# A retention-and-feed-forward kernel: v of the first two batches loaded as bf16 by partition quarters and put in order on TensorE, and two blocks of the first product begun by halves

## The chip, the cores and the metric

The kernel runs on one core of one Trainium2 chip. The metric is device time in microseconds (us) of one execution; the time of a kernel is the median of several executions. A core has five engines with queues of their own: TensorE (PE, whose weight loads are listed apart as PEld), VectorE (DVE), ScalarE (ACT), GpSimd (POOL) and SyncE (SP). They run side by side and wait for one another through semaphores. Transfers are issued on POOL or SP and carried out by 16 DMA engines. Matrix products read their operands from the on-chip memory SBUF (128 partitions) and write to the accumulators in PSUM.

## The reference

```python
def _attn_ref(q, k, v):                      # (8 batches, 8 heads, 576 tokens, 64)
    scores = 1.0 / np.sqrt(64) * np.matmul(q, k.transpose(0, 1, 3, 2))
    gamma = 1.0 - 2.0 ** (-5.0 - np.arange(H))
    Dmat = np.where(rel >= 0, gamma[:, None, None] ** rel, 0.0)   # rel = row - column
    return np.matmul(scores * Dmat, v)

def _moe_ref(x, w_in, w_out):                # x (4608, 512), w_in (512, 2048), w_out (2048, 512)
    h = x @ w_in
    sp = np.where(h > 20.0, h, np.log1p(np.exp(np.minimum(h, 20.0))))
    return (h * np.tanh(sp)) @ w_out

def reference(q, k, v, moe_w_in, moe_w_out):
    x = _attn_ref(q, k, v).transpose(0, 2, 1, 3).reshape(B * S, H * D)
    return _moe_ref(x, moe_w_in, moe_w_out)
```

Each head is attention with a decay in place of a softmax: the weight of token j for token i is the score times gamma to the power i - j. Because nothing is normalised, a chunk of tokens can be computed from its own scores and a running state, the sum of k times v over the tokens before it. The result goes through two products with the function Mish between them.

## The kernel before

The 4608 tokens are cut into 36 chunks of 128, and four chunks make a tile of 512 tokens, so there are nine tiles. The first two tiles are the first 128 tokens of batches 0 to 3 and of batches 4 to 7; the other seven hold the rest in order. For every tile the kernel makes xT, the attention output with features on the partitions (4 x 128 features by 512 tokens). Then comes G1: sixteen blocks f (`g1`), each four products of 128x128 weights from w_in with 512 columns of xT, summed in a PSUM bank named hp, after which ACT applies Mish and writes gT. Then G2 (`g2_first`, `g2`): for each chunk, sixteen products of gT with w_out, summed, copied and stored. The attention work of a later tile is laid between the products of an earlier one. The order on every engine is written out by hand, and each engine's queue is in order: an instruction that waits holds all behind it.

Tile 0 has nothing before it that could cover its attention work, so the kernel begins with a stretch in which TensorE has little to do. It runs as follows (line numbers of the kernel before).

- POOL issues the loads of k, q and v of batches 0 to 3 (`load_first_qk`, L106; `load_first_v`, L117) and of w_in (`load_w_in`, L86), in the order written; SP issues q of batches 0 and 1. q and k come eight tokens to a row, 128 rows to a batch, and are cast to bf16 on the way, except on SP, which brings fp32. v comes as fp32 in pairs of batches, one token to a partition, 16 pieces of 64 values in each. Between the first loads POOL fills the tables of indices (L129 to L137) from which DVE makes the exponents of the decay (`dmask`, L150), the unit matrix (`ident`, L152) and `ex` (L600). ACT takes the exponentials (L598 to L602).
- `keep_warm` runs products of zeros on TensorE; their results are not used.
- `f_transpose` (L193, copies at L198) turns q and k of a pair of batches; `f_scores` (L212) multiplies them and DVE multiplies by the decay (L216, tile sm).
- `f_v` (L226) casts v to bf16 on ACT, POOL or DVE; `f_out` (L242) multiplies it with the masked scores, and a copy writes xT (L246), the last one on DVE.
- G1 of tile 0 begins (L513; with `halved` set, some products are split into two of 256 columns, L518).

While G1 of tile 0 runs, POOL scales v of batches 0 to 3 by the decay (`f_state`, L254, tile v0s), which with k of the same tokens (`cast_k0`, L262, cast from fp32) later gives the first state of each batch (L388). POOL's loads use eight semaphores in turn, so that a load's issue waits for the landing of the load eight before it.

## Time and profile before

| | |
|---|---|
| median of 3 runs | 301.16 us (300.12 to 302.53) |
| profiled execution | 301.52 us, of which span 299.7 us |
| busy share: DVE / ACT / POOL | 46% / 45% / 46% |
| moved by DMA | 47.44 MB, mean 158 GB/s |
| first product of G1 | at 17.02 us |
| v of batches 0, 1 | issued at 5.74 us, 6.97 us to landing |
| v of batches 2, 3 | issued at 6.93 us, 7.9 us to landing |

The span is the time from the first to the last instruction of one profiled execution; the execution's own time lies 1.8 us above it. The profile's page lists busy time by engine, the span in forty slices, the DMA queues, the chain of work that ended last, the costliest groups of instructions and the DMA issues. Groups read as: line, engine, operation, written tile, read tiles, shapes, count, then busy time and mean length. The trace answers further questions: who waited for whom, the instructions in order of time, and busy time by stretch. Ends of matmuls are modelled, so the start times of matmuls are the firmer numbers.

### The profile page before, as it was taken

To read this page: it belongs to the slowest core of one execution; us is meant where nothing else is said; L and a number is where in the kernel's file an instruction comes from. 1 tells how busy PE (TensorE), PEld (TensorE's weight loads), DVE (VectorE), ACT (ScalarE), POOL (GpSimd) and SP (SyncE) were. 2 spreads that over 40 slices of the span, in tenths; PEclk is the share of its full clock that TensorE was granted. 3 is DMA by queue.
4 is the path that set the end of the run, shared out by engine and by line. 5 is a ranking of instruction groups with operands and counts; after the bars stand their busy time and mean duration, and the time that the engine had idled before them with its cause. 6 is when DMAs were issued, how large, how long until landed. Compare 5 with 4: busy or idle time off the path is not lost.

```text
span 299.7 us, 7937 instructions
## 1 busy us (share of the span) xinstructions
PE 289.6 (97%) x3454; PEld 158.0 (53%) x3492; DVE 136.9 (46%) x234; ACT 135.1 (45%) x221; POOL 136.9 (46%) x184
## 2 busy tenths in 40 slices
PE   8889999999999999999999999999999999999995
PEld 3456787555455545456655454545454544444443
DVE  5813447597839527462646453536373312010011
ACT  5657226876557553534363434343435342433200
POOL 8596846767474297190927555817440000000000
PEclk9999999999999999999999999999999999999999
DMA  7999999999999649999897989797922110110121
GB/s 153 210 206 205 205 238 220 338 221 203 245 227 225 139 137 205 169 188 190 198 189 176 181 155 231 136 214 168 191 72 70 37 37 35 37 35 35 52 90 70
DMA packets 39618, 47.44 MB, mean 158 GB/s; under 512 B 21792, under 2 KB 28448, under 8 KB 39584
## 3 DMA queue, kind: packets, MB, share of 16 engines
q0 software_dynamic: 14896, 32.25, 51.6%
q1 hardware_dynamic: 24544, 14.49, 22.6%
q8 instruction: 27, 0.44, 0.7%
q10 hardware_dynamic: 144, 0.20, 0.2%
q14 instruction: 7, 0.06, 0.1%
HBM read 38.80 MB, written 9.44 MB: 161 GB/s over the span
## 4 chain that ended last, share of the span: by engine, by line
PE 92%; DMA 2%; issue 2%; POOL 2%; ACT 0%; DVE 0%; POOLq 0%
PE hp L513 41%; PE ops L513 30%; PE hp L518 6%; PE ops L518 3%; DMA gT<-in_v_dram 2%; PE sc L333 2%; PE hp L464 1%; PE sc L313 1%; PE sc L388 1%; PE hp L447 1%; PE hp L573 1%; PE st L518 1%; POOL gT L106 1%; PE st L388 1%; PE sc L190 1%
## 5 line engine op out<-in xcount | busy, mean ns | idle before, releaser
L513 PE MATMUL hp<-xT,w_in_t 128*128 128x512 bf16 (+1 forms) x508 | 127.8, 377 | 1.4 <-DVE gqk L650 0.3
L529 ACT ACTIVATE gT<-hp 128x512 bf16<-128x512 f32 x144 | 86.2, 599 | 92.2 <-PE hp L513 87.6
L513 PE MATMUL ops<-w_out_t,gT 128*128 128x512 bf16 x412 | 102.0, 379 | 2.0 <-issue 1.9
L513 PEld LDWEIGHTS <-w_in_t 128*128 128x128 bf16 x526 | 51.1, 98 | 54.8 <-issue 1.5
L513 PEld LDWEIGHTS <-gT 128*128 128x128 bf16 x480 | 45.7, 98 | 52.2
L581 DVE COPY res<-ops 128x512 f32<-128x512 f32 x28 | 19.3, 690 | 92.4 <-PE ops L513 92.4
L294 DVE TENSOR_TENSOR qks<-qkraw,gqk 128x512 bf16<-128x512 f32 x56 | 36.8, 714 | 3.6 <-DMA qkraw<-in_k_dram 3.6
L482 POOL COPY held<-qkT 128x1 bf16<-128x1 bf16 x18 | 5.4, 299 | 59.8 <-DMA qkT<-qks 59.8
L275 POOL DMA_DIRECT2D qkraw<-in_q_dram x24 | 21.4, 890 | 11.7 <-ACT gT L529 8.0
L275 POOL DMA_DIRECT2D vraw<-in_v_dram x24 | 21.2, 883 | 3.8 <-DMA vpair<-in_v_dram 3.0
L275 POOL DMA_DIRECT2D qkraw<-in_k_dram x24 | 21.2, 883 | 2.7 <-DMA w_out_t<-in_moe_w_out_dram 1.5
L476 DVE CAST xT<-hp 128x512 bf16<-128x512 f32 x13 | 9.0, 692 | 27.4 <-PE hp L464 19.7
L476 ACT CAST xT<-hp 128x512 bf16<-128x512 f32 x14 | 8.2, 586 | 29.0 <-PE hp L464 20.5
L301 POOL TENSOR_TENSOR vs<-vraw,gv 128x512 bf16<-128x512 f32 x18 | 18.9, 1075 | 1.2 <-PE hp L447 1.1
L424 DVE TENSOR_TENSOR total<-sc,total 128x256 f32<-128x256 f32 x40 | 16.9, 422 | 1.0
L339 DVE TENSOR_TENSOR sm<-sc,mask 128x1024 bf16<-128x1024 f32 x14 | 17.0, 1216 | 0.7 <-PE sc L333 0.7
L518 PEld LDWEIGHTS <-gT 128*128 128x128 bf16 x160 | 15.3, 98 | 3.2
L518 PE MATMUL hp<-xT,w_in_t 128*128 128x256 bf16 x108 | 16.2, 273 | 0.0
L518 PEld LDWEIGHTS <-w_in_t 128*128 128x128 bf16 x108 | 10.5, 98 | 6.5
L427 ACT CAST ssb<-total 128x768 bf16<-128x768 f32 (+3 forms) x13 | 11.7, 898 | 1.7 <-DVE total L424 1.6
L513 PE MATMUL hp<-w_out_t,gT 128*128 128x512 bf16 x49 | 12.0, 379 | 0.2 <-issue 0.2
L518 PE MATMUL ops<-w_out_t,gT 128*128 128x256 bf16 x76 | 10.0, 273 | 0.1
(118 smaller groups left out, 254.8 us busy)
## 6 DMA issues: line engine op xcount, KB each, us to landing
out_dram<-res SPq DMA_DIRECT2D x31, 256.0 KB, 4.3
qkraw<-in_q_dram POOLq DMA_DIRECT2D x24, 256.0 KB, 6.6
qkraw<-in_k_dram POOLq DMA_DIRECT2D x24, 256.0 KB, 6.9
vraw<-in_v_dram POOLq DMA_DIRECT2D x24, 256.0 KB, 7.7
w_out_t<-in_moe_w_out_dram POOLq DMA_DIRECT2D x4, 512.0 KB, 11.1
k0r<-in_k_dram POOLq DMA_DIRECT2D x8, 256.0 KB, 5.8
w_in_t<-in_moe_w_in_dram POOLq DMA_DIRECT2D x3, 512.0 KB, 9.4
gT<-in_k_dram POOLq DMA_DIRECT2D x8, 128.0 KB, 6.5
```

Of the source, the lines that this page charges most:

```text
L275: ins = nc.gpsimd.dma_start(out=t, in_=src[b, :, ds(P * c, P), :].rearrange("h p d -> p h d"))
L294: nc.vector.tensor_tensor(slots[:, :, y], heads[:, :, y], factors[:, :, y].unsqueeze(3).to_broadcast([P, NP, 2, D]), op=OP.mult)
L301: engine.tensor_tensor(vs, live[n]["v"], gv[:, c, :].unsqueeze(2).to_broadcast([P, H, D]), op=OP.mult)
L333: nc.tensor.matmul(sc[i, e, x, p, :], lhsT=qk[r, 1, p, i], rhs=qk[r, 0, p, i], start=True, stop=True, skip_group_check=True)
L339: nc.vector.tensor_tensor(sm.rearrange("p e x n i -> p (e x n) i"), live[n]["sc"].rearrange("p e x n i -> p (e x n) i"), mask.unsqueeze(1) ...
L424: nc.vector.tensor_tensor(new[:, k], st[:, j, x], total[b], op=OP.add)
L427: casts.append(lambda copy: copy(lows[:, 0:k], new[:, 0:k]))
L476: copy(xts[t][:, :, ds(P * s, 2 * P)].rearrange("p h (x j i) -> p j h x i", x=2, j=2)[:, j], both[j])
L513: nc.tensor.matmul(to, lhsT=w, rhs=x, start=first, stop=last)
L518: nc.tensor.matmul(to[:, ts(j, n)], lhsT=w, rhs=x[:, ts(j, n)], start=False, stop=False, skip_group_check=True)
L529: done = nc.scalar.activation(gts[t][:, f, :], hp, AX.Mish)
L581: copy(ot, ops)
```

## The change

There are five parts to it.

1. v of batches 0 and 1 is no longer loaded as one fp32 pair but by four loads (`load_four_tokens`), one for each quarter of the 128 partitions. Each brings four of the sixteen head rows, with four tokens (1 KB of fp32) to a run, cast to bf16 on the way: 256 KB are written in all instead of 512.
2. In that layout a partition holds four neighbouring tokens of one head instead of one token of all heads. `f_v_spread` puts the tokens in order on TensorE: for each quarter four products with 32 rows, whose weights `spread` are a matrix with a one where token t belongs, made by DVE in `make_spread` from a new table `apart`. ACT copies the four results (256 columns each) to `spread_v`. These products and copies stand around and inside `f_scores` of the second pair of batches, and that of the first pair moves ahead of the second transposes of k.
3. v of batches 2 and 3 is cast by POOL alone. Most products of zeros are left out (10, 1 and 2 remain of 12, 2, 3, 3, 4 and 2).
4. `g1_half` computes the first 256 columns of G1's blocks 0 and 1, which need only batches 0 and 1, ahead of the loop; the loop then does the second halves. Blocks 2 to 4 are not split any more.
5. `spread_v` itself serves as v0s of batches 0 and 1; the decay is put on k instead, so that `cast_k0` of these two is a DVE product and two `f_state` products of POOL go.

Besides, constants are made in another order, `ex` is one product instead of eight, the exponential of `dmask` is taken in two halves, and fp32 q of batch 1 is cast by a product with a column of ones.

```diff
@@ -96,6 +96,7 @@
     gts = {0: gp.tile([P, nF, NCH * P], BF16, name="gT")}
     q0 = gts[0][:, H:nF, :].bitcast(F32).rearrange("p (b a) c -> p b (a c)", a=2)
     v0 = {}
+    v0s = {}
     fst = {}
 
     def load_first_qk(t, i, b):
@@ -105,6 +106,15 @@
             fst[t] = {"qb": stage[:, 0:4, :], "kb": stage[:, 4:8, :], "vb": {}}
         nc.gpsimd.dma_start(out=fst[t][name][:, b, :],
                             in_=(q, k)[i][4 * t + b, :, 0:P, :].rearrange("h (g r) d -> g h (r d)", r=8))
+
+    spread_v = first.tile([P, 2, H, D], BF16, name="v01")
+    v0s[0], v0s[1] = spread_v[:, 0], spread_v[:, 1]
+
+    def load_four_tokens(e):
+
+        nc.gpsimd.dma_start(out=stage[ds(32 * e, 32), 8:10, :].rearrange("p b (x c) -> p (b x) c", x=2),
+                            in_=v.rearrange("b h s d -> (b h) s d")[e:2 * H:4, 0:P, :]
+                            .rearrange("j (g r) d -> g j (r d)", r=4))
 
     def load_first_v(b):
 
@@ -125,34 +135,54 @@
     nc.vector.memset(zeros, 0.0)
     lnd = consts.tile([P, 1], F32)
     nc.vector.memset(lnd, -0.5 * math.log(D))
+    one = consts.tile([P, 1], F32)
+    nc.vector.memset(one, 1.0)
+    lg = [math.log(1.0 - 2.0 ** (-5.0 - h)) for h in range(H)]
+    lgr = consts.tile([P, H], F32)
+    for h in range(H):
+        nc.vector.memset(lgr[:, h:h + 1], lg[h])
+    quarter = consts.tile([P, 4], F32)
+    for e in range(4):
+        for r in range(4):
+            nc.vector.memset(quarter[ds(32 * e, 32), r:r + 1], r - 128.0 * e)
+    gqk = consts.tile([P, 5, 2, H], F32)
+    nc.vector.memset(gqk, 1.0)
     dist = consts.tile([P, P], F32)
     nc.gpsimd.iota(dist, pattern=[[1, P]], base=0, channel_multiplier=-1,
                    allow_small_or_imprecise_dtypes=True)
     nc.gpsimd.affine_select(out=dist, in_=dist, compare_op=OP.is_ge, fill=1.0e6,
                             base=0, pattern=[[1, P]], channel_multiplier=-1)
     ident = consts.tile([P, P], BF16)
+    load_first_qk(0, 1, 2)
     pos = consts.tile([P, 5], F32)
     nc.gpsimd.iota(pos, pattern=[[P, 5]], base=0, channel_multiplier=1,
                    allow_small_or_imprecise_dtypes=True)
     nc.gpsimd.iota(pos[64:P, 4:5], pattern=[[1, 1]], base=512, channel_multiplier=1,
                    allow_small_or_imprecise_dtypes=True)
-    for i in (1, 0):
-        for b in (2, 3):
-            load_first_qk(0, i, b)
-    load_first_v(0)
+    load_first_qk(0, 1, 3)
+    apart = gts[0][:, 0, 0:2 * P].bitcast(F32)
+    nc.gpsimd.iota(apart, pattern=[[1, P]], base=0, channel_multiplier=-4, allow_small_or_imprecise_dtypes=True)
+    for b in (2, 3):
+        load_first_qk(0, 0, b)
+    for e in range(4):
+        load_four_tokens(e)
     load_first_v(2)
     for f0, n in ((0, 256), (256, 256), (512, 512)):
         load_w_in(f0, n)
     mask = consts.tile([P, 64], F32)
-    lg = [math.log(1.0 - 2.0 ** (-5.0 - h)) for h in range(H)]
     dmask = consts.tile([P, H, P], F32)
+    ex = consts.tile([P, 5, H], F32)
     for h in range(H):
         nc.vector.tensor_scalar(dmask[:, h, :], dist, lg[h], None, op0=OP.mult)
-    ex = consts.tile([P, 5, H], F32)
     nc.vector.tensor_scalar(ident, dist, 0.0, None, op0=OP.is_equal)
-
-    gqk = consts.tile([P, 5, 2, H], F32)
-    nc.vector.memset(gqk, 1.0)
+    nc.vector.tensor_tensor(ex, pos.unsqueeze(2).to_broadcast([P, 5, H]),
+                            lgr.unsqueeze(1).to_broadcast([P, 5, H]), op=OP.mult)
+    spread = gts[0][:, 1, :].rearrange("p (r t) -> p r t", r=4)
+
+    def make_spread(rs):
+        for r in rs:
+            nc.vector.tensor_scalar(spread[:, r, :], apart, quarter[:, r:r + 1], None, op0=OP.is_equal)
+
     gq = gqk[:, :, 0, :]
     gv = consts.tile([P, 5, H], F32)
     warm = consts.tile([P, 1], F32)
@@ -165,7 +195,6 @@
     xts = {}
     k0 = {}
     k0r = {}
-    v0s = {}
 
 
     def f_mix(g, i):
@@ -198,13 +227,15 @@
             copy(to, src)
         fst[t][name, g] = out_t
 
-    def f_scores(t, g):
+    def f_scores(t, g, between=None):
 
         qT, kT = fst[t]["qb", g], fst[t]["kb", g]
         scs = [ps_sc.tile([P, 2, NP, P], F32, name="sc") for _ in range(2)]
         for x in range(2):
             fst[t]["sm", 2 * g + x] = first.tile([P, H, P], BF16, name="sm0", bufs=4)
         for hs in (0, NP):
+            if hs and between:
+                between()
             for h in range(hs, hs + NP):
                 for x in range(2):
                     r = ds(64 * x, 64)
@@ -218,6 +249,21 @@
                 elif hs > 0:
                     nc.vector.tensor_tensor(sm, scs[x].rearrange("p a b i -> p (a b) i"), dmask, op=OP.mult)
 
+    def f_v_spread(es, banks, copy):
+
+        rows = stage[:, 8:10, :].rearrange("p b (x r d) -> p b x r d", x=2, r=4)
+        for e, (pool, name) in zip(es, banks):
+            to = pool.tile([P, 2, 2, 2, D], F32, name=name)[:, 0]
+            for r in range(4):
+                nc.tensor.matmul(to, lhsT=spread[ds(32 * e, 32), r, :], rhs=rows[ds(32 * e, 32), :, :, r, :],
+                                 start=(r == 0), stop=(r == 3))
+            copies.append((spread_v.rearrange("p b (x e) d -> p b x e d", x=2)[:, :, :, e, :], to))
+        for to, src in copies:
+            copy(to, src)
+        copies.clear()
+
+    copies = []
+
     def f_v(t, b, copy):
         vb = first.tile([P, H, D], BF16, name="vb", bufs=4)
         copies = copy if isinstance(copy, tuple) else (copy,)
@@ -229,7 +275,7 @@
     def f_out(t, b, copy):
         if b == 0:
             xts[t] = xp.tile([P, KC, NCH * P], BF16, name="xT")
-        vb = fst[t]["vb"][b]
+        vb = v0s[b] if t == 0 and b < 2 else fst[t]["vb"][b]
         if t == 0:
             pool, name = ((ps_h, "hp"), (ps_h, "hp"), (ps_st, "st"), (ps_o, "ops"))[b]
             ot = pool.tile([P, NP, P], F32, name=name)
@@ -250,7 +296,7 @@
     def f_state(t, b, engine=nc.gpsimd):
 
         n = 4 * t + b
-        v0s[n] = first.tile([P, H, D], BF16, name="v0s", bufs=B)
+        v0s[n] = first.tile([P, H, D], BF16, name="v0s", bufs=B - 2)
         engine.tensor_tensor(v0s[n], v0[n], gv[:, 0, :].unsqueeze(2).to_broadcast([P, H, D]), op=OP.mult)
 
     def load_k0(b):
@@ -259,7 +305,10 @@
 
     def cast_k0(b, copy=nc.scalar.copy):
         k0[b] = first.tile([P, H, D], BF16, name="k0", bufs=3)
-        copy(k0[b], k0r[b])
+        if b < 2:
+            nc.vector.tensor_tensor(k0[b], k0r[b], gv[:, 0, :].unsqueeze(2).to_broadcast([P, H, D]), op=OP.mult)
+        else:
+            copy(k0[b], k0r[b])
 
 
 
@@ -518,12 +567,20 @@
             nc.tensor.matmul(to[:, ts(j, n)], lhsT=w, rhs=x[:, ts(j, n)], start=False, stop=False,
                              skip_group_check=True)
 
-    def g1(t, f, parts=1):
+    def g1_half(f):
+        hp = ps_h.tile([P, NCH * P], F32, name="hp")
+        n = NCH * P // 2
+        for c in range(KC):
+            nc.tensor.matmul(hp[:, 0:n], lhsT=w_in_t[:, c, ts(f, P)], rhs=xts[0][:, c, 0:n],
+                             start=(c == 0), stop=(c == KC - 1))
+        return hp
+
+    def g1(t, f, parts=1, begun=None):
         if t not in gts:
             gts[t] = gp.tile([P, nF, NCH * P], BF16, name="gT")
-        hp = ps_h.tile([P, NCH * P], F32, name="hp")
+        hp = ps_h.tile([P, NCH * P], F32, name="hp") if begun is None else begun
         n = NCH * P // parts
-        for j in range(parts):
+        for j in range(0 if begun is None else 1, parts):
             for c in range(KC):
                 product(hp[:, ts(j, n)], w_in_t[:, c, ts(f, P)], xts[t][:, c, ts(j, n)], c == 0, c == KC - 1)
         done = nc.scalar.activation(gts[t][:, f, :], hp, AX.Mish)
@@ -595,41 +652,39 @@
     dve, act, pool = nc.vector.tensor_copy, nc.scalar.copy, nc.gpsimd.tensor_copy
 
 
-    nc.scalar.activation(dmask, dmask, AX.Exp, bias=lnd[:, 0:1])
-    for h in range(H):
-        nc.vector.tensor_scalar(ex[:, :, h], pos, lg[h], None, op0=OP.mult)
+    for j in range(2):
+        part = dmask[:, ds(NP * j, NP), :]
+        nc.scalar.activation(part, part, AX.Exp, bias=lnd[:, 0:1])
     nc.scalar.activation(gq, ex, AX.Exp)
     nc.scalar.activation(gv, ex, AX.Exp, scale=-1.0)
     nc.scalar.activation(warm, lnd, AX.Mish)
-    for b in range(2):
-        dve(fst[0]["qb"][:, b, :], q0[:, b, :])
-    keep_warm(12)
+    dve(fst[0]["qb"][:, 0, :], q0[:, 0, :])
+    nc.vector.tensor_tensor(fst[0]["qb"][:, 1, :], q0[:, 1, :], one.to_broadcast([P, H * D]), op=OP.mult)
+    make_spread((0, 1))
+    keep_warm(10)
     f_transpose(0, 0, 1, [(ps_h, "hp", act), (ps_h, "hp", dve)])
     f_transpose(0, 0, 0, [(ps_st, "st", act), (ps_o, "ops", dve)])
-    keep_warm(2, ps_sc, "sc")
+    make_spread((2, 3))
+    keep_warm(1, ps_sc, "sc")
+    f_scores(0, 0)
     f_transpose(0, 1, 1, [(ps_h, "hp", act), (ps_h, "hp", act)])
-    f_scores(0, 0)
     f_transpose(0, 1, 0, [(ps_st, "st", act), (ps_o, "ops", act)])
-    f_v(0, 0, pool)
-    f_v(0, 1, act)
+    f_v_spread((0, 1), ((ps_h, "hp"), (ps_h, "hp")), act)
+    f_scores(0, 1, lambda: f_v_spread((2, 3), ((ps_st, "st"), (ps_o, "ops")), act))
+    f_v(0, 2, pool)
+    f_v(0, 3, pool)
     load_w_in(1024, 512)
-    keep_warm(3, ps_h, "hp")
-    f_scores(0, 1)
-    keep_warm(3)
+    load_w_in(1536, 512)
     f_out(0, 0, act)
     f_out(0, 1, act)
-    keep_warm(4, ps_st, "st")
-    f_v(0, 2, (act, pool))
-    f_v(0, 3, dve)
-    load_w_in(1536, 512)
     f_out(0, 2, act)
     f_out(0, 3, dve)
     keep_warm(2, ps_sc, "sc")
+    begun = [g1_half(0), g1_half(1)]
     for i, b in ((1, 0), (1, 1), (0, 0), (0, 1)):
         load_first_qk(1, i, b)
     for i in range(2):
         load_w_out(i)
-        f_state(0, i)
     for i, b in ((1, 2), (1, 3), (0, 2), (0, 3)):
         load_first_qk(1, i, b)
     for b in (2, 3):
@@ -650,8 +705,10 @@
     nc.vector.tensor_scalar(gq, gq, 1.0 / math.sqrt(D), None, op0=OP.mult)
 
 
-    for f in range(nF):
-        halved[0] = 2
+    for f in range(2):
+        g1(0, f, 2, begun[f])
+    for f in range(2, nF):
+        halved[0] = 2 if f > 4 else 0
         g1(0, f)
     for i in range(2):
         f_mix(0, i)
```

## The prediction

> **What bounds the kernel now.** I read the page first: parts 1 and 2 for the bounding engine, then the chain of waits for what holds the start, then the list of waits, the sums by stretch and the timeline of the first 20 us.
>
> ```profile
> PE 289.6 (97%) x3454; PEld 158.0 (53%) x3492; DVE 136.9 (46%) x234; ACT 135.1 (45%) x221; POOL 136.9 (46%) x184
> ...
> PEclk9999999999999999999999999999999999999999
> ```
>
> TensorE is busy nearly always, at full granted clock in every slice. After 17 us the list of waits names for PE nothing but short issue gaps (1.9 us in 12 pieces the longest entry), so the stretch after 17 us is matmul time, and the change touches almost none of it. What can move is the start:
>
> ```profile
> 3.58 2.16 POOL gT L106 x4
> 5.74 6.97 DMA gT<-in_v_dram
> 12.84 0.62 POOL vb L226
> ...
> 13.97 1.07 ACT xT L246 x2
> ...
> 15.40 0.52 PE st L242 x8
> 15.92 0.24 PE ops L242 x8
> 16.19 0.69 DVE xT L246
> ...
> 17.02 0.38 PE hp L513
> ```
>
> This is the chain of waits (start, length, what): POOL's issues, the transfer of v for batches 0, 1, its cast, the output products, the copy to xT, and at 17.02 the first product of G1. The columns of the next view are length, busy time of PE, PEld, DVE, ACT and POOL, granted clock, DMA share and GB/s:
>
> ```profile
> 11.00:13.00 2.00, 1.41 (x20) 0.69 (x19) 2.00 (x4) 0.41 (x2) 0.16 (x1) 1.00 1.04 223
> 13.00:15.00 2.00, 1.65 (x21) 0.79 (x20) 1.46 (x4) 1.39 (x4) 1.25 (x3) 1.00 1.36 188
> 15.00:17.00 2.00, 1.24 (x18) 0.63 (x19) 1.09 (x3) 0.93 (x3) 2.00 (x4) 1.00 1.35 205
> 17.00:20.00 3.00, 2.98 (x21) 2.02 (x22) 0.00 (x0) 1.37 (x3) 3.00 (x5) 1.00 1.24 207
> ```
>
> Before 17 us PE has holes, partly filled with products of zeros; the DMA share is full. The transfers set the pace: v of batches 0, 1 lands at 12.7 (5.74 + 6.97), v of 2, 3 at 14.9 (issued 6.93, 7.9 to landing). Both feed the casts:
>
> ```profile
> POOL vb L226 <- DMA gT<-in_v_dram: 3.2, 2, 2.5
> ACT vb L226 <- DMA gT<-in_v_dram: 1.6, 1, 1.6
> DVE vb L226 <- DMA gT<-in_v_dram: 0.5, 1, 0.5
> ```
>
> So I price the change by when v of 2, 3 lands, and what follows from there to G1.
>
> **Issues on POOL.** A q or k load of 128 rows holds POOL 0.53 to 0.55 us; the v load with 2,048 rows 1.2. A quarter has 128 rows of 1 KB, so 0.53 each: 2.1 in place of 1.2. The new index fill costs 0.3 (the row of the other one), and k of batch 2 goes ahead of two fills. Adding up from 3.25: k2 3.25, k3 4.1, q2 4.9, q3 5.4, quarters 5.9 to 7.9, v of 2, 3 at 7.9 instead of 6.93, first w_in 9.1 instead of 8.09. POOL's loads use eight semaphores in turn, so each waits for the landing of the one eight earlier; the three extra loads move v of 2, 3 behind k2 (landed 7.0) and the third w_in behind q3 (9.6, issue at 10.6): no cost. Two scalings of v (L254, 1.09 and 1.06) go from POOL at 19 to 21 us, where nothing waits: worth nothing.
>
> **The transfers.** The old load of 0, 1 writes 512 KB; it took 3.1 from q3's landing (9.6) to its own; the load behind it 2.15. The quarters write 256 KB as bf16. No row shows a 32-partition load. The nearest, the w_in blocks of 256 columns, also 512 runs of 1 KB cast to bf16, took 1.0 and 1.6 from landing to landing (14.9, 15.9, 17.45); I take 1.35, or 0.34 a quarter. v of 0, 1 is then there at 10.95. v of 2, 3 follows by 2.15 to 3.1: 13.1 to 14.05. Counted from its later issue with the 6.97 of the first v load it would be 14.9, but that 6.97 includes waiting behind q3. I take 13.8, nearest the middle of these bounds: **1.05 earlier**.
>
> **From the landing to G1.** Before: batch 2 cast by ACT and POOL halves, 3 by DVE (0.43), and f_out of batch 3 ends at 16.14, 1.28 after landing. After: POOL casts both alone, 0.61 each (row of batch 0), then 0.39 of products and about 0.1 of handing over: 1.75, so 0.47 lost. Then PE had to wait 0.88 for the last xT copy (0.69 on DVE). Now it runs two zero products (0.43) and the two half blocks: four 256-column products take 0.44 in the chain, so 0.87. These 1.30 cover the 0.88. The 0.87 is work taken from blocks 0 and 1, so G1 counts as begun 0.43 after f_out: 13.8 + 1.75 + 0.43 = 15.98, against 17.02: **1.04 gained**. Blocks 0 and 1 in halves still take 0.87 each; blocks 2 to 4 unsplit take 0.86 (L513 x4 in the chain) for 0.87: 0.03. Without the halves the xT wait would be late instead, 0.45 worse.
>
> **The other inputs to f_out.** q of batch 1 is converted by a product, 0.7 in place of 1.07 at 6.15; the four spread masks cost DVE 0.15 to 0.22 each (rows L150, L152), two of them ahead of its first copy. Scores of pair 0 start at 8.7 (8.95 before) and move ahead of the second k transposes. ACT gets four copies of 256 columns (0.42 at most, row L226) and loses two casts (0.62, 0.42). PE gets 16 products of 256 columns, 0.11 each, or up to 0.16 if their weight loads (0.1) don't overlap; bounds 1.75 to 2.6, I take 1.75, and 13 zero products of 0.21 go. Laid out by these rows the last spread copy ends near 13.5, the last masked score (0.61 each, eight in line from 9.15, second half after the spread products) near 14.8, f_out of batch 3 near 15.4. By v of 2, 3 it is 15.55. So **this chain has only 0.15 to spare**: if v came earlier than 13.65, the masked scores would be late next.
>
> **Behind G1's start.** The w_in blocks come 1.0, 1.6 and 2.3 apart: 14.8, 16.4, 18.7, needed at 16.0, 17.7 and 19.4. The fourth is issued behind both casts (15.1 instead of 13.4), while the third still fills the queue. The DMA front moves by about what PE gains, so later slack stays (v of 4 to 7 lands at 46.7, its product at 47.9). Scaling k of batch 0 moves from ACT (0.63) to 0.71 of DVE at 55 us, hidden by 1.49 of DVE waiting for k; uncovered it would cost 0.7. Batch 1's grows by 0.1, beside 0.67 of idle time.
>
> **Sum.** −1.04 − 0.03 = −1.07. The profiled execution took 301.52 (span 299.7 and 1.8 around it): 300.45. The median of the runs is 0.36 lower: **300.1**.
>
> **Rivals.**
> (a) *The later issue eats it.* v of 2, 3 needs its full 6.97: landing 14.9, G1 at 17.05, time 301.1. For it: v queued almost dry at 8.5 to 9 (150 GB/s from 8 to 9 against 253 from 9 to 12). Against: that wait was partly q3's.
> (b) *Slower: a quarter is a bad shape.* Break-even is a landing of 14.84, 0.6 a quarter. At 0.85, near the 1.0 of a whole 256 KB block, v of 2, 3 lands 2.0 later than I take it, at 15.8, G1 at 18.0: 302.1. Against it: cast loads already run at some 205 GB/s in every stretch, as though the cast bounds them, not the destination. [...]
> (c) *The clock.* Zero products at the start take 0.43 each (12 in 4.98) and later 0.21: half rate for 4.5 us. With 13 fewer of them a second such stretch costs up to 2.25: 302.3. Against: the granted clock stays 1.00 from 11 to 17 us with PE 62 to 83% busy, and real products fill the places. [...]
> (d) *More.* v at 13.1 and the masked scores 0.6 sooner than laid out: G1 at 15.3, 299.4.
> (e) The change does what it says in every case: the order of instructions on each engine shows it.
>
> **Chances.** Forecast (299.7 to 300.7) 0.50, (a) 0.17, (b) 0.13, (c) 0.07, (d) 0.10, something unnamed 0.03. The range 299.2 to 301.8 takes in the forecast, (a), (d) and the mild end of (b). One per cent, 3.0 us, is about what a measurement here can tell (the three runs lie 2.4 apart); no case reaches it, so within 1% gets 0.92, faster 0.03, slower 0.05 for the worst of (b) and (c).
>
> **What will show it.** Quarters issued at 5.9 to 7.9, 0.53 each; v of 2, 3 issued near 7.9 and landed near 13.8; POOL casts of 0.61 behind it; half blocks before the last xT copy ends; the first product of G1 near 16.0 and the second halves near 16.85. I am wrong if v lands at or after 14.8, if f_out waits for DVE's masked scores instead, if w_in holds block 2 or 4, or if matmuls after 16 us are 0.43 apart.

## The result and the profile after

The changed kernel is slower: 310.63 us in the median (308.51 to 313.26, 4 executions) against 301.12 (300.12 to 302.53), a ratio of 1.029 with a 95% interval of 1.024 to 1.035. Its profiled execution took 311.14 us, span 309.4: 9.6 more than that of before. (Ratios leave out executions over 1.5% above the fastest of the same kernel; for the three kernels below without a ratio, only the median, the lowest and highest execution and the profile are given.)

From the page of after: busy time by engine, the granted clock by slice, and the engines' shares of the chain that ended last.

```profile
PE 291.9 (94%) x3456; PEld 159.5 (52%) x3493; DVE 137.4 (44%) x256; ACT 134.9 (44%) x223; POOL 135.6 (44%) x186
...
PEclk9959999999999999999899999999999999999999
...
PE 84%; DMA 10%; POOL 2%; issue 2%; DVE 0%; POOLq 0%; SPq 0%
```

The shares of the chain before:

```profile
PE 92%; DMA 2%; issue 2%; POOL 2%; ACT 0%; DVE 0%; POOLq 0%
```

There the chain had 2% of DMA, and the clock row was all nines. Now DMA has 10%, and the clock row has a 5 in slice 3 and an 8 in slice 20. Those are the two places where time went. TensorE's list of waits has an entry for each:

```profile
PE sc L382 <- DMA qkT<-qks: 4.3, 2, 3.2
PE st L288 <- POOL vb L272: 2.7, 1, 2.7
```

**First place: the start.** The chain up to G1 (start, length, what):

```profile
6.35 2.14 POOL gT L115 x4
8.49 7.47 DMA gT<-in_v_dram
...
16.02 0.62 POOL vb L272
...
16.68 0.64 PE st L288 x8
17.32 0.56 PE ops L288 x8
...
18.63 1.91 PE hp L574 x8
```

The four quarters are issued by 8.49; their last one landed at 11.30. v of batches 2, 3, issued at 8.49, landed at 15.96 (before: 14.86). Its casts and output products follow, and the first half block of G1 begins at 18.63. The sums by stretch show what the wait did (length, busy PE, PEld, DVE, ACT, POOL, then granted clock, DMA share, GB/s):

```profile
13.00:15.00 2.00, 0.92 (x16) 0.54 (x16) 1.62 (x3) 1.40 (x4) 0.00 (x0) 1.00 1.28 180
15.00:17.00 2.00, 0.32 (x6) 0.32 (x8) 0.00 (x0) 0.00 (x0) 0.98 (x2) 0.69 1.35 199
17.00:20.00 3.00, 2.78 (x23) 1.74 (x20) 0.78 (x2) 0.58 (x1) 3.00 (x6) 0.50 1.02 145
20.00:25.00 5.00, 5.00 (x24) 2.71 (x23) 0.00 (x0) 2.39 (x4) 2.59 (x5) 0.74 1.19 193
```

TensorE has 0.92 of 2 us between 13 and 15 and 0.32 between 15 and 17; then the granted clock is 0.50. By the trace's clock events (the times at which the granted clock changed) it fell at 15.75 and came back at 22.58. So G1 begins 1.61 later than before (18.63 against 17.02) and runs its first 3.95 us at half rate, which loses 1.97: 3.58, and indeed block 8 of tile 0 is 3.56 behind before.

**Second place: 147 us.** That lag stays at 3.3 to 3.7 us up to tile 4, then grows to 8.6 there and to 9.7 in tile 5. The chain around it, and the sums by stretch:

```profile
138.56 13.20 DMA qkT<-qks
...
151.80 0.32 PE sc L382 x16
```

```profile
149.00:152.00 3.00, 0.20 (x24) 0.20 (x28) 1.90 (x3) 0.00 (x0) 0.12 (x1) 1.00 0.86 157
152.00:155.00 3.00, 2.83 (x73) 1.95 (x62) 1.82 (x2) 0.58 (x1) 2.72 (x4) 0.55 0.57 135
```

In the later tiles q and k are transposed by DMA, issued by SP. This transpose took 13.2 us to land; the same one of before was issued at 134.93 and took 7.8. From the rows on qkT between 100 and 200 us, before and then after:

```profile
DMA to landing us min/median/max: 3.1/7.4/9.9
```

```profile
DMA to landing us min/median/max: 3.2/7.5/13.2
```

TensorE waited 3.23 us for it, and then again the clock was halved, for 3.41 us. A second wait of 1.1 us follows at 185. The change touches nothing within 70 us of these.

### The profile page after: what moved, and what is told of

It reads as the page before. It is cut to its first block, busy times and chain, and to the rows that moved or that the text cites. A ratio compares the mean times of both kernels' runs of the same rounds, so it can differ in the third digit from the quotient of the medians.

```text
span 309.4 us, 7967 instructions
## 1 busy us (share of the span) xinstructions
PE 291.9 (94%) x3456; PEld 159.5 (52%) x3493; DVE 137.4 (44%) x256; ACT 134.9 (44%) x223; POOL 135.6 (44%) x186
## 4 chain that ended last, share of the span: by engine, by line
PE 84%; DMA 10%; POOL 2%; issue 2%; DVE 0%; POOLq 0%; SPq 0%
PE hp L562 38%; PE ops L562 27%; DMA qkT<-qks 8%; PE hp L567 5%; DMA gT<-in_v_dram 2%; PE ops L567 2%; PE sc L382 1%; PE sc L362 1%; PE hp L513 1%; PE sc L437 1%; PE hp L630 1%; PE st L567 1%; PE hp L496 1%; POOL gT L107 1%; POOL gT L115 1%
## 5 line engine op out<-in xcount | busy, mean ns | idle before, releaser
L562 PE MATMUL hp<-xT,w_in_t 128*128 128x512 bf16 (+1 forms) x518 | 130.0, 380 | 1.6 <-issue 0.8
L531 POOL COPY held<-qkT 128x1 bf16<-128x1 bf16 x18 | 4.5, 248 | 66.6 <-DMA qkT<-qks 66.6
L324 POOL DMA_DIRECT2D qkraw<-in_q_dram x24 | 21.3, 889 | 13.8 <-ACT gT L586 9.5
L567 PE MATMUL hp<-xT,w_in_t 128*128 128x256 bf16 x88 | 13.2, 273 | 0.0
L382 PE MATMUL sc<-qkT 64*64 64x64 bf16 x448 | 7.2, 196 | 4.3 <-DMA qkT<-qks 4.3
```

The lines of the kernel that those rows point to most:

```text
L324: ins = nc.gpsimd.dma_start(out=t, in_=src[b, :, ds(P * c, P), :].rearrange("h p d -> p h d"))
L382: nc.tensor.matmul(sc[i, e, x, p, :], lhsT=qk[r, 1, p, i], rhs=qk[r, 0, p, i], start=True, stop=True, skip_group_check=True)
L562: nc.tensor.matmul(to, lhsT=w, rhs=x, start=first, stop=last)
L567: nc.tensor.matmul(to[:, ts(j, n)], lhsT=w, rhs=x[:, ts(j, n)], start=False, stop=False, skip_group_check=True)
```

## The experiments

### Does the start's loss come from the clock, and the later loss from the start?

The change brought three small constants (`one`, `lgr`, `quarter`). By the compiled programs each takes 32 bytes of every partition, so all tiles allocated behind the constants lie 96 bytes higher than before. The first two kernels bear on that: before with tiles 32 bytes higher, and after with tiles 64 bytes higher than before.

```diff
+    shim = consts.tile([P, 1], F32)
+    nc.vector.memset(shim, 0.0)
     dist = consts.tile([P, P], F32)
```

> The kernel before with one more 32-byte constant, so that every tile behind the constants starts at 32 past a multiple of 64 bytes, as in the changed kernel; no work is changed. Theory A (the second loss of the changed kernel, 5 us near 150 us and 1 near 185, where PE waits for the DMA transposes, comes from the tiles' addresses): 306 to 307. Theory B (it comes from the later start and the order of the transfers): 301.1, no change.

302.55 us (300.30 to 304.67), ratio 1.005 (1.001 to 1.009); waits for qkT of 1.5 us in all. The time lies between the two forecasts.

```diff
-    one = consts.tile([P, 1], F32)
-    quarter = consts.tile([P, 4], F32)
+    quarter = consts.tile([P, 5], F32)
+    one = quarter[:, 4:5]
```

> The changed kernel with its constant one put into the tile quarter, so that every tile behind starts at a multiple of 64 bytes, as in the kernel before; no work is changed. Theory A: the loss near 150 to 185 us goes, 304 to 305 is left (the 3.5 us lost before the first block of G1 ends). Theory B: 310, no change against the changed kernel.

309.40 us (307.90 to 312.57), ratio 1.027 (1.022 to 1.031): about as after. Waits for qkT come to 5.0 us.

The next lays zero products into the hole of after (the 2.7 us in which TensorE waits for the casts of v), the one behind it joins both edits.

```diff
     f_out(0, 1, act)
+    keep_warm(12, ps_st, "st")
     f_out(0, 2, act)
```

> The changed kernel with twelve products of zeros (12 x 0.21 = 2.6 us) between the output products of batch 1 and batch 2, where PE stood idle for 2.7 us. Theory C (the clock went to half from 15.75 to 22.6 us because of that hole): clock 1.00 throughout, first Mish at about 19.2 instead of 21.5, 2.3 us gained at the start. With the clock kept, and v of batches 2, 3 still landing at 16, the start is 1.1 us behind the kernel before. If the second loss is a consequence of the start, 302; if not, 308.

314.03 us (306.78 to 318.11). The clock came up at 10.0 us instead of 5.5 and did not fall in the start; G1's blocks are 2.16 us behind before instead of 3.56. But the waits for qkT come to 7.7 us, and TensorE stands 2.17 us at 82 us with no releaser named ("issue").

> Both edits at once: tiles at multiples of 64 bytes and twelve products of zeros in the hole. Theories A and C together: 302.2, the later landing of v of batches 2, 3 alone being left. If A is wrong: as the run with the zero products alone.

313.26 us (310.76 to 313.92), ratio 1.040 (1.035 to 1.045). Blocks 2.41 behind; an issue gap of 3.26 us at 83; waits for qkT 4.1.

So the fall of the clock is a part of the start's loss, and the later waits do not follow from it. I also took it from these runs that addresses are not the cause, since 64 bytes in place of 96 had changed nothing. That was wrong, as the last group shows.

### A late start, more instructions, the moved scalings, the half blocks

Before with a late G1:

```diff
     f_out(0, 3, dve)
-    keep_warm(2, ps_sc, "sc")
+    keep_warm(20, ps_sc, "sc")
```

> Before, with 18 more zero products of 512 columns behind the last f_out, so that G1 begins some 3.4 us later with TensorE never idle (18 x 0.216 = 3.9, of which about 0.45 lies in the wait for the last copy to xT). Nothing else differs, but TensorE has 36 instructions more. Theory L (a late start is enough to bring the later waits for the DMA transposes, because the transfers of the first 45 us are late by less than TensorE is): 307 to 313 us, with waits of 1 to 4 us for qkT between 130 and 190 us. Rival S or N (the later waits come from something else in the change): 300.8 + 3.4 = 304.2 us, within 1 us, no wait for qkT over 0.5.

308.15 us (307.04 to 309.10), ratio 1.024 (1.018 to 1.030). No wait for qkT. The blocks are 3.33 late, and the rest is one gap and the half clock behind it, in the chain of waits:

```profile
78.76 0.75 PE ops L513 x3
79.52 3.38 issue
82.90 2.29 PE ops L513 x5
```

Before with as many instructions more, at no work (`cols` is the width of a zero product):

```diff
-    keep_warm(12)
+    keep_warm(24, cols=256)
...
-    keep_warm(4, ps_st, "st")
+    keep_warm(8, ps_st, "st", 256)
...
-    keep_warm(2, ps_sc, "sc")
+    keep_warm(4, ps_sc, "sc", 256)
```

> Before, with the first 12 zero products made 24 of 256 columns, and the last 4 and 2 made 8 and 4 of 256: the same zero columns, 36 more TensorE instructions, as in the run with the late start, at no time to speak of (0.11 each, at most 0.3 us in all for weight loads that don't overlap). Theory R (where TensorE's instruction blocks are fetched decides whether it stalls, as in the two runs with 24 more instructions that had gaps of 2.2 and 3.3 us near 83 us): a gap of 1 us or more that before does not have, named as issue, 302 to 309 us. Otherwise 300.8, within 1 us.

305.89 us (303.78 to 309.80), ratio 1.014 (1.006 to 1.022), with the same gap (3.41 us at 75.9) and no wait for qkT.

A late start does not bring the waits, then; and 36 more TensorE instructions that take no time bring a gap of 3.4 us. The issue gaps of the two runs with fillers look alike. In the packet records one queue of instructions, which I take to be TensorE's (the trace does not name it), arrives in pieces of 16 KB, around 80 us every 4 to 7 us and near the end 27 apart. That the place of the pieces decides on the gap is my reading, not shown; a gap of 1.0 us near 75 us also stands in the run with three loads more below, which has TensorE's instructions of before. After's own longest gap of this kind is 0.5 us against 0.2 before.

After with v of batches 0, 1 scaled in place on POOL, and k only cast:

```diff
     for i in range(2):
         load_w_out(i)
+        f_state(0, i)
...
-        if b < 2:
-            nc.vector.tensor_tensor(k0[b], k0r[b], gv[:, 0, :].unsqueeze(2).to_broadcast([P, H, D]), op=OP.mult)
-        else:
-            copy(k0[b], k0r[b])
+        copy(k0[b], k0r[b])
```

> After, with the scalings of v of batches 0 and 1 back on POOL behind the w_out loads (in place, on the bf16 v) and k of batches 0 and 1 only cast, on ACT and DVE, as in before. The start is untouched: G1 some 3.4 us late. Theory S (the moved scalings upset the order of transfers and copies later): the later waits go, 304 to 305 us. Rivals L and N: no change against after, 308 to 313 us, with waits for qkT of 1 us or more behind 120 us.

309.96 us (305.41 to 315.75), ratio 1.020 (1.010 to 1.030). Not the moved scalings: a transpose of 13.9 us, a wait of 2.2. The edit leaves the start as in after, yet in this profiled execution the clock did not fall there (v of 2, 3 landed at 14.85; the clock came up only at 10.7), and the start cost 0.4 us; the later loss was 3.7. So after's 3.6 us at the start is not lost in every execution.

Before with the half blocks alone:

```diff
     keep_warm(2, ps_sc, "sc")
+    begun = [g1_half(0), g1_half(1)]
...
-    for f in range(nF):
-        halved[0] = 2
+    for f in range(2):
+        g1(0, f, 2, begun[f])
+    for f in range(2, nF):
+        halved[0] = 2 if f > 4 or f == 2 else 0
         g1(0, f)
```

> Before, with only the half blocks of the change: the first 256 columns of G1's blocks 0 and 1 run ahead of the last copy to xT, blocks 3 and 4 unsplit; TensorE's count of instructions is the same. By the prediction's step (0.45 of the wait for xT covered, 0.02 for the unsplit blocks) 300.3 us, the first Mish 0.4 us earlier than 18.09, no new wait. If every small shift of TensorE against the transfers brings waits for qkT of 1 us or more (a strong form of theory L): 302 or more.

301.09 us (300.16 to 302.45), ratio 0.999 (0.997 to 1.002). The first Mish came 0.18 earlier, no more than it differs between traces of the same start (0.1 to 0.5). The second came 0.55 earlier and the third 0.20: with two blocks begun side by side in the two hp banks, the third has to wait for the Mish that empties a bank, and the cover is mostly given back there.

```profile
18.56 0.38 PE L513 MATMUL hp<-xT,w_in_t 128*128 128x512 bf16 x1 [0.25 <-ACT gT L537]
```

In the profiled execution (302.45, the highest of the ten) TensorE also waited for qkT, 1.9 us in two pieces, though all tiles lie where before has them.

### The order of the loads, their number, and when they meet the transposes

After with v of batches 2, 3 loaded first:

```diff
+    load_first_v(2)
     for e in range(4):
         load_four_tokens(e)
-    load_first_v(2)
```

> After, with the load of v of batches 2, 3 issued ahead of the four quarters. If the late landing of v of 2, 3 (15.96 us, 7.5 behind its issue at 8.49) is what opens the hole in which the clock falls, it now lands at 12.7 to 13.3, as the first v load of before did (12.71), the quarters at 13.5 to 14.5, PE waits for the quarters at most some 1.5 us and the granted clock stays 1.00 from 11 to 20 us: first Mish 17.7 to 18.7, against 21.49. If any order leaves a hole (the transfers as a whole end at the same time), the clock falls again and the first Mish comes after 20.5. The later waits are not touched: 1 to 6 us of waits for qkT, or of issue gaps, in either case, so 303 to 307 us with a warm start and 307 to 312 with a cold one.

314.00 us (308.71 to 319.85), ratio 1.028 (1.017 to 1.038). v of 2, 3 landed at 13.47, but the quarters then at 13.73 to 14.75, and TensorE waited for them instead:

```profile
PE hp L258 <- DMA gT<-in_v_dram: 3.2, 1, 3.2
```

The clock fell at 13.09, and the first Mish came at 21.54. Whichever goes first, the last of v is there at about 15 to 16 us (14.86 before), though 256 KB less are written. A wait for qkT of 2.0 us and an issue gap of 1.1 follow later.

Before with three loads more, and before with POOL's loads held back behind every second transpose:

```diff
+    for b in range(3):
+        nc.gpsimd.dma_start(out=zeros[:, ds(D * b, D)], in_=q[0, 0, 0:P, :])
     for b in range(4):
         load(N0 + b)
```

> Before, with three loads of 128 rows more (one head of q, written over the zeros, which nothing reads any more) on POOL's queue at some 38 us, so that the count of loads ahead of the chunks is that of after. Theory Q (the three loads more shift the turn of the eight semaphores or the place in the ring, and so the later meeting of loads and DMA transposes): waits for qkT of 1.5 us or more in all, 303 to 307 us. Rival: no wait that before does not show, 300.8 to 301.5 us.

302.28 us (300.34 to 308.79), ratio 1.002 (0.997 to 1.006), no wait for qkT.

```diff
         nc.gpsimd.tensor_copy(held[:, n % 2:n % 2 + 1], live[n]["qk"][:, 1, NP - 1, P - 1:P])
+        if n % 2:
+            nc.gpsimd.tensor_copy(zeros, zeros)
```

> Before, with a copy of the zeros (512 wide, some 0.6 us on POOL) behind each second copy that holds POOL until a DMA transpose has landed, so that the loads behind it are issued 0.6 us later against TensorE and against the next transpose. In after, the loads of 131 us came 0.60 later than in before and met the transpose issued then: 11.8 and 13.2 us to landing in place of 7.8. Theory M (the later waits are such meetings: a few tenths of a us between POOL's loads and the transpose decide whether both take 4 to 8 us or 10 to 15): one or more waits for qkT of 1 us or more, 302 to 310 us. Rival: the loads have slack, 300.8 to 301.5 us, landings as in before.

301.00 us (300.22 to 304.55), ratio 1.001 (0.997 to 1.005), no wait for qkT; at 112 us the loads began 2.4 us ahead of the transpose instead of 2.7.

That distance seemed to go with a transpose's time in the traces so far, so the next two kernels set it alone (one copy, then two), and the third mends the start of after: zero products in the hole, the casts of v of 2, 3 split over three engines as in before, and the last w_in load behind them.

```diff
                 load_k0(2 * t - 2 + i // 8)
+                if t == 3 and i == 4:
+                    for _ in range(1):
+                        nc.gpsimd.tensor_copy(zeros, zeros)
```

> Before, with one copy of the zeros (0.6 us on POOL) between the load of k0 and the six loads behind it at 109.6 us, so that these reach the DMA transpose issued at 112.3 about 0.6 us closer: the row of seven loads then stands as if it began 2.1 us ahead of the transpose in place of 2.7. In the traces so far that transpose took 6.9 to 9.2 us where the loads began 2.6 or 2.7 ahead, 9.7 to 11.7 at 2.4 and 2.5, and 12.0 to 15.0 at 2.0 to 2.3. Theory M2 (that distance sets it): 12 us or more for this transpose, 10 or more for the next, a wait of PE for qkT of 1 to 3 us by 135 us, 302 to 306 us. Rival (the distance only goes along with something else in those kernels): 8 to 9 us to landing, no wait, 300.8 to 301.5.

301.27 us (300.01 to 305.05), ratio 1.000 (0.996 to 1.003). That transpose took 8.6 us where 12 or more was expected, and no wait followed: the distance alone is not the cause.

> The same with two copies (1.2 us), as if the loads began 1.5 us ahead of the transpose. By the rows of other places (1.2 and 1.4 ahead: 6.1 and 6.5 us) theory M2 expects 6 to 9 us to landing and no wait, 300.8 to 301.8; if later is simply worse, 12 us or more and a wait, 302 to 307.

303.17 us (300.62 to 306.68), ratio 1.006 (1.003 to 1.009). That one took 6.9 us, the next but one 13.6, and waits for qkT of 1.7 in all followed, again with all tiles where before has them. Moving loads costs something, but not 2%.

```diff
-    f_v(0, 2, pool)
-    f_v(0, 3, pool)
...
     f_out(0, 1, act)
+    keep_warm(10, ps_st, "st")
+    f_v(0, 2, (act, pool))
+    f_v(0, 3, dve)
...
-        halved[0] = 2 if f > 4 else 0
+        halved[0] = 2 if f > 9 else 0
```

> After, with the start mended: ten zero products between f_out of batches 1 and 2, the casts of v of batches 2, 3 split over ACT, POOL and DVE as in before, and five G1 blocks fewer with a halved product, so that TensorE's count of instructions is that of after. No hole: granted clock 1.00 from 11 us on, first Mish at 18.0 to 19.2 (before 18.09, after 21.49). If all later loss follows from the hole in the start: 300.5 to 302.5 us. Theory M2 (the later meetings depend on tenths of a us and not on the hole): waits for qkT of 1 us or more remain in the profile, 302 to 309.

313.40 us (308.32 to 321.87). The start is mended, though v of 2, 3 landed at 15.55: the first Mish came at 18.77, 0.68 behind before. These are the stretches that had clocks of 0.69 and 0.50 in after:

```profile
15.00:17.00 2.00, 1.94 (x23) 0.93 (x22) 0.55 (x2) 0.75 (x2) 1.40 (x3) 1.00 1.35 198
17.00:20.00 3.00, 2.70 (x21) 1.94 (x20) 0.66 (x2) 1.33 (x3) 2.83 (x5) 1.00 1.25 206
```

And still, from TensorE's waits:

```profile
PE sc L382 <- DMA qkT<-qks: 8.3, 2, 6.0
```

The later loss stands on its own: 10 us in this execution (312.43), with the clock at full rate through the start.

### What is left: the quarters or the addresses

The mended version with v of batches 0, 1 loaded whole (and zero products in place of those that sort it):

```diff
-    for e in range(4):
-        load_four_tokens(e)
+    load_first_v(0)
     load_first_v(2)
...
+    for b, copy in ((0, pool), (1, act)):
+        copy(spread_v[:, b], v0[b])
     load_w_in(1024, 512)
```

> The version with the mended start (312 to 313 us), with v of batches 0, 1 loaded whole as in before and cast by POOL and ACT, and 16 zero products of 256 columns where the products that put the quarters in order were; constants, masks, halves, the moved scalings and TensorE's count of instructions stay. Theory Q2 (the quarter loads themselves, by their 512 pieces of 1 KB in place of 2,048 of 256 B or by their three loads more, upset the loads and transposes 100 us later): no wait for qkT of 1 us or more, 300.5 to 302.5. Rivals (addresses, constants, or the moved scalings): waits of 2 us or more in all, 305 or more.

308.03 us (307.18 to 311.13), ratio 1.023 (1.014 to 1.032); a transpose of 14.2 us, a wait for qkT of 2.5 (besides, the clock was half from 8.8 to 12.2 us and the start 2.0 late). It is not the quarters.

The last three move addresses only. Where the tiles lie, by the compiled programs (byte in each partition):

```
                             qkraw    qks     qkT     res    modulo 256
before, mended/old           96128  130944  144256  219008      128
after, mended, before + 96   96224  131040  144352  219104      224
mended, 128 lower            96000  130816  144128  218880        0
```

The mended version with the new constants in a part of gT that is not yet in use:

```diff
+    small = gts[0][:, 2, 0:32].bitcast(F32)
-    one = consts.tile([P, 1], F32)
+    one = small[:, 0:1]
...
-    lgr = consts.tile([P, H], F32)
+    lgr = small[:, 1:1 + H]
-    quarter = consts.tile([P, 4], F32)
+    quarter = small[:, 9:13]
```

> The version with the mended start, with the new constants (1, the logarithms, the quarter offsets) put into a part of gT that is not yet in use, so that weights, q, k, v, qks, qkT and all other tiles of the steady part lie at the very addresses that they have in before (in after 96 bytes higher). Theory A2 (the address itself, not its place within 64 bytes, sets how the DMA transposes and loads meet): no wait for qkT of 1 us or more, 300.5 to 302.5. Rivals (quarter loads, moved scalings): waits of 2 us or more in all, 305 or more.

303.96 us (301.48 to 312.50), ratio 1.007 (1.004 to 1.010): above the 302.5 expected, but with no wait for qkT. From the rows on qkT between 100 and 200 us, issue to landing, first the mended version at after's addresses, then at those of before:

```profile
DMA to landing us min/median/max: 3.6/7.7/15.9
```

```profile
DMA to landing us min/median/max: 3.1/6.5/8.7
```

What it still loses in the profiled execution is the start (0.6) and an issue gap at 212 us, the largest piece of this entry of its waits:

```profile
PE ops L563 <- issue: 4.8, 13, 2.9
```

Besides that edit, `ex` in gT too and a larger constant:

```diff
-    ex = consts.tile([P, 5, H], F32)
+    ex = small[:, 16:16 + 5 * H].rearrange("p (c h) -> p c h", h=H)
...
-    held = consts.tile([P, 2], BF16)
+    held = consts.tile([P, 18], BF16)
```

> The version with the mended start and the constants in gT, in which the early table of exponents goes to gT too and a constant is made larger, so that every tile of the steady part lies 128 bytes lower than in before: not at its addresses, but at multiples of 128 bytes as there. (The runs with tiles 32, 64 and 96 bytes off a multiple of 128 all had waits for qkT.) Theory A128 (a place at a multiple of 128 bytes is what counts): no wait for qkT of 1 us or more, 302 to 304.5 us, as with the old addresses. Theory A2 (the very address counts): waits of 2 us or more in all, 306 to 313.

302.61 us (300.79 to 307.35), ratio 1.005 (1.001 to 1.009). No wait for qkT in the profiled execution: it need not be the very address.

Before, with nothing but an unused constant:

```diff
+    shim = consts.tile([P, 24], F32)
+    nc.vector.memset(shim, 0.0)
     dist = consts.tile([P, P], F32)
```

> Before, with an unused constant of 96 bytes, so that all later tiles lie where after has them, 96 bytes higher; nothing else differs. Theories A128 and A2 (the address alone brings the later waits): waits for qkT of 2 us or more in all behind 110 us, 303 to 310 us, with the start as in before. If it takes the change's other parts too: no wait of 1 us or more, 300.8 to 302.

311.45 us (302.33 to 314.03). Three of the four executions took 310.38 to 314.03, as long as the whole change; the fourth took 302.33 at full clock, which is within what before takes (299.97 to 304.86 in the 14 executions beside it). The profiled one took 314.03, with its start as it was (first Mish 0.47 earlier). From TensorE's waits there:

```profile
PE sc L335 <- DMA qkT<-qks: 9.5, 3, 6.0
```

So the shift alone can bring the waits into before, but not in every execution, and this kernel gives no size for it. The pair of mended versions does: at after's addresses the two lowest of the four executions took 308.32 and 312.43, at the old ones eight of ten took 301.48 to 304.79 (the other two, 306.75 and 312.50, have no profile, so what they lost is open). The twenty profiled executions, sorted by where the tiles lie:

| tiles, against before | modulo 256 | executions | longest transpose between 100 and 200 us | waits of TensorE for qkT in all |
|---|---|---|---|---|
| as before | 128 | 9 | 7.8 to 13.6 us | none in seven; 1.7 and 1.9 in two |
| 128 lower | 0 | 1 | 11.0 | none |
| 32 higher | 160 | 1 | 11.9 | 1.5 |
| 64 higher | 192 | 2 | 12.7 and 13.0 | 5.0 and 4.1 |
| 96 higher | 224 | 7 | 13.2 to 16.0 | 2.0 to 9.5 |

Waits of 2 us or more stand in all nine with tiles 64 or 96 bytes higher and in none of the other eleven. With the pair of mended versions that shows the cause at the second place: the addresses bring the large waits. How they do it stays open (last section). Small ones come at the old addresses too, so the 1.5 us at 32 bytes cannot be put down to the shift. By the medians 64 bytes cost about 5 us (309.40 less the start's 3.2), and 96 about 6 in after and 9 with the start mended, where single executions lie 13 us apart.

## Why the prediction was wrong

Forecast 300.1 in a range of 299.2 to 301.8; it became 310.6. The terms, for the profiled execution:

| step of the prediction | forecast | measured |
|---|---|---|
| quarters landed, v of 0, 1 there | 10.95 | 11.30 |
| v of 2, 3 issued | 7.9 | 8.49 |
| v of 2, 3 landed | 13.8 | 15.96 |
| from there to the end of f_out of batch 3 | 1.75 | 1.92 |
| zero products ahead of G1 | 0.43 | 0.75 |
| G1 begun | 15.98 | 18.63 |
| clock after that | full | half for 3.95 us: 1.97 lost |
| behind G1's start | -0.03 | +6.1 |

The clock was half from 15.75 on, so the 1.92 and the 0.75 hold a part of its price as well.

**Issues on POOL.** The issue of k of batch 3 and the index fill took 1.19 together instead of 0.8, the four quarters 2.17 instead of 2.0. Mis-sized by 0.6.

**The transfers: the step that failed first.** The quarters were priced rightly: 0.33 to 0.41 from landing to landing, 0.34 forecast. So rival (b), the bad shape, which broke even at 0.6, fell. The four were in flight together, and no run here times a quarter alone. What failed is "v of 2, 3 follows by 2.15 to 3.1". It followed by 4.7, and by 2.8 to 4.3 in the variants. I had taken intervals between landings of transfers that were in flight together for the time one of them needs. Rival (a) was nearest to what the runs show: v of 2, 3 takes its time from issue, 6.0 to 7.5 us in all these runs, with the quarters ahead of it or behind, and landed at 14.5 to 16.0 behind the quarters, against 14.86 before. The reversed order did not help either: the last of v then landed at 14.75.

**The clock.** Rival (c), at 0.07, is what happened, in after, with the tiles 64 bytes higher and with the loads in the other order. Its price was nearly right (2.25 forecast, 1.97 measured), partly by luck: the half rate lasted 6.83 us instead of the 4.5 assumed, and 3.95 of them fell on G1. Wrong was the argument against it, "real products fill the places": between 13.97 and 16.68 there were none, because the work that was to fill the place was done before the late transfer came. With ten zero products there and the casts split (the mended start) the clock stayed at 1.00 from 11 to 25 us. The clock events of after lie at 5.51, 15.75 and 22.58 us: 10.24 and 6.83 apart, three and two times the 3.41 that the fall at 152.29 lasted. The time at which the clock first came up differs between the runs (5.1 to 10.7 us). What sets these times was not shown.

**The half blocks** were to cover the wait for the last copy to xT, and 0.45 was forecast for that. In after they began at 18.63, when that copy (17.92 and 0.69 long) had just ended, so they covered nothing. In before alone they did begin ahead of its end (16.41 against 16.76), but the third block's wait for a bank, 0.25, was not priced, and the time did not change.

**"Later slack stays": the step that cost most.** The prediction weighed the order of the work and held its slack for kept, and up to 147 us it was: no new wait. It put the DMA transposes behind that at nothing and left out where the tiles lie. Three constants, 13 numbers in each partition, put everything behind them 96 bytes higher, and by the pair of mended versions (313.40 and 303.96) the loss behind G1's start comes from that; before with the shift alone showed it in three executions of four. None of the rivals had it; the 0.03 for something unnamed was all that stood for it. The 6.1 is that of one execution of after: the price differs from one execution to the next.

With the start mended and the tiles put back, what is left of the change is 302.6 to 304.0 us: in the profiled executions 0.6 to 1.1 later at the start, with v of 2, 3 landing at 14.53 and 15.32 against 14.86, and issue gaps of 1.6 to 2.9 at 212 us. No version was faster than before.

## What to carry to other kernels

Before a change is priced, compare the addresses of the large tiles in both kernels: one more constant can move them all, and the cost then shows far from the edit (here three constants, 96 bytes: 313.40 us with the start mended, 303.96 with the tiles put back; the first wait for qkT in after stood at 149 us, 70 us from anything the change touches); if they moved, put the constant elsewhere, so that they lie as before. A filler product may be taken out only if real work stands in the same microseconds even when the transfer before it is late: in after TensorE was busy for 1.24 of the 4 us from 13 to 17 and the clock was half for 6.83; with ten zero products there, 3.75 of 4, it stayed at 1.00. And the interval between two landings is not the time of the second transfer when both were in flight: before, v of 2, 3 landed 2.15 us behind v of 0, 1, but 7.9 behind its issue.

## What the hardware showed that was not expected

**Loads were faster in the one kernel with the tiles at multiples of 256 bytes.** With the tiles 128 bytes lower, loads of fp32 without a cast ran at half as much again, in the stretch where they are nearly all that moves. Sums by stretch, of before and then of the mended version 128 bytes lower (last column GB/s):

```profile
41.00:43.00 2.00, 2.00 (x23) 1.68 (x20) 1.23 (x1) 1.01 (x1) 0.57 (x1) 1.00 1.01 217
43.00:45.00 2.00, 2.00 (x31) 1.71 (x30) 1.29 (x2) 0.67 (x2) 0.47 (x1) 1.00 1.04 221
```

```profile
41.00:43.00 2.00, 2.00 (x28) 1.89 (x27) 0.91 (x1) 0.48 (x1) 1.06 (x2) 1.00 1.04 346
43.00:45.00 2.00, 2.00 (x30) 1.56 (x29) 0.55 (x2) 2.00 (x4) 1.37 (x2) 1.00 1.02 334
```

In the packet records, packets of 4,096 bytes between 42 and 51 us take 195 ns in the median there and 308 in before, and 308 as well in the mended version at before's addresses, so it is not the mended start; between 54 and 57, with stores among them, they take 179 in both. The profile pages' rows on loads and stores (issue to landing) show it less clearly, before and then 128 lower:

```profile
out_dram<-res SPq DMA_DIRECT2D x31, 256.0 KB, 4.3
qkraw<-in_q_dram POOLq DMA_DIRECT2D x24, 256.0 KB, 6.6
```

```profile
out_dram<-res SPq DMA_DIRECT2D x31, 256.0 KB, 2.4
qkraw<-in_q_dram POOLq DMA_DIRECT2D x24, 256.0 KB, 5.8
```

The stores' 2.4 is the lowest of all runs (2.7 to 4.5 in the others), the q loads' 5.8 is not (5.7 to 7.2).

This does not explain the transposes: between 35 and 75 us the median packet of 4,096 bytes takes 304 to 307 ns in all runs but that one, so these packets do not tell tiles 32, 64 or 96 bytes higher from those of before. How a shift of 64 or 96 bytes brings the waits remains open: shown is only that the address decides (waits of 2 us or more in all nine executions with tiles 64 or 96 bytes higher, in none of the other eleven), and for multiples of 256 by one kernel. Also not tried is before with its tiles at multiples of 256 bytes.

**Instructions that cost nothing where they stand can cost elsewhere.** 36 TensorE instructions more, at no work in the start, brought a gap of 3.41 us near 76 us for which the trace names no releaser, and the clock was halved from 78.37 us on, for 6.83.
